# A new order of units in a block-sorted attention and gated MLP kernel

## The chip, the cores and the metric

The kernel runs on one core of a Trainium2 chip. The metric is device time in microseconds (us) of one execution. Before the change the median of three runs is 159.92 us (159.0 to 159.92). An engine here is one of TensorE (PE, with its weight loads as PEld), VectorE (DVE), ScalarE (ACT), GpSimd (POOL) and SyncE (SP, which in this kernel only starts DMAs). Each engine takes its instructions in the order in which the program wrote them, and waits on semaphores for what the others make.

## The reference

Two stages, four batches, eight heads, 768 tokens of 64 values, eight blocks of 96 tokens. The matrix P (8 x 8 for each batch and head) is normalised five times over rows and columns; K and V are mixed over blocks with P; each block of queries attends to its own mixed block. A gated MLP follows.

```python
for _ in range(5):                       # P: [B, H, 8, 8]
    P = np.exp(P - P.max(-1, keepdims=True))
    P = P / P.sum(-1, keepdims=True)
    P = P / P.sum(-2, keepdims=True)
k_sorted = einsum('bhij,bhjcd->bhicd', P, k_blocks)
v_sorted = einsum('bhij,bhjcd->bhicd', P, v_blocks)
attn = softmax(q_blocks @ k_sorted.T / 8)      # inside each block
x = (attn @ v_sorted) as [B, 768, 512]
h = relu(x @ w_in);  u, v = h[..., :512], h[..., 512:]
v_n = (v - mean(v)) / sqrt(var(v) + 1e-6)
gated = u * (w_spatial @ v_n + b_spatial)
out = gated @ w_out
```

## The kernel before

The whole program is one list of short units, the string `ORDER`. The program walks through the list and each word calls one function `u_<name>` with the arguments behind the colons. The place of a word in the list sets the place of its instructions in the queue of every engine that it uses; nothing reorders them later. The first number of most words is the PSUM bank that the unit writes (eight banks; a unit takes the bank and the one behind it), and the letter is the engine that empties it: A for ScalarE, D for VectorE, P for GpSimd.

The words, with the line of the work in the profile:

- `L:x:b`, `LH`: loads of q, k, v of batch b, and of the weights (`wv`, `wu`: the two halves of w_in; `ws`: w_spatial; `wo`: w_out). GpSimd writes them and casts float32 to bfloat16 on the way (lines 156, 165, 204 to 212).
- `SK`, `PR`, `P0`, `PC`, `PD`: P is normalised on a 32 x 64 tile, spread over 128 partitions on TensorE, and multiplied by a 0/1 mask into the mixing weights `pd` of a batch: for batch 0 by VectorE (`P0`, line 269), for the others by GpSimd (`PD`, line 281) from a copy (`PC`).
- `QT`, `KT`: q is transposed, k mixed and transposed, one pair of heads at a time (lines 324 and 339; a copy out of PSUM at line 108 or 110).
- `VT`, `VX`: batch 0 only. V is mixed like K (line 339), copied out, and turned back (line 378) into `vb`. The last argument of `VT` is 0 or 1 for one half of the blocks (64 columns) and 2 for all blocks at once (128 columns).
- `VM`, `VC`: the other batches. V is mixed with tokens on partitions into `vm` (line 390), and SyncE moves it into `vb` with one DMA for each block, four DMAs for each half of the blocks (line 405).
- `SC`, `AT`: scores and exp (lines 423 and 436), then attention times V (line 448) and the division (lines 459 and 460), for a batch, a pair of heads and a half `ih` of the blocks. `AT:...:P` sends the product through a ScalarE copy (line 456) to GpSimd.
- `XT`, `XX`: x is transposed, for batch 0 on TensorE, later by a DMA transpose of SyncE. `QX` (batches 2 and 3) arranges q, on VectorE (line 181) or GpSimd (line 179), and transposes it by such a DMA (line 183).
- `VP`, `LN`, `LA`: the v half of w_in, relu, mean and variance (lines 491, 114 or 116, 505, 506), the reciprocal root, and the normalisation on VectorE (line 525) or GpSimd (lines 521, 522).
- `UP`: the u half (line 536). `WS`: w_spatial transposed (line 297). `SP`, `SH`: the product with w_spatial (line 548; line 568 in halves), the bias (lines 554, 573) and the gate (lines 560, 577). `OP`, `OH`: w_out and the store (lines 597, 583).
- `DM`: products of a tile of zeros that nobody reads, early in the program (line 290).

`WT:q:2` is a copy of one element of the turned q of batch 2 on GpSimd (line 305). The loads of batch 3 stand behind it in GpSimd's queue, so they cannot start before that DMA transpose has landed. Buffers rotate: two each for q, k, v and `vb`, four for exp results, two for `z` (which `AT:...:P` shares), two and three for outputs.

Of the kernel before, what the change touches and what calls it, by code (L numbers as in the profile page):

```python
# [13 lines left out]


ORDER = """
IN SK:0 LH:q:0:0:4 L:k:0:0:128 ID MK SK:0 L:v:0:0:128 SK:0 QT:0:A:0:1:2 SK:0 QT:2:A:0:0:2 DM:0:12:64
LH:q:0:4:8 DM:1:12:64 SX L:wv DM:0:12:64 DM:1:12:64 SK:1 DM:0:12:64 DM:1:12:64 PR:0 P0:1:4:8 IV:1
P0:0:4:8 P0:1:0:4 P0:0:0:4 DM:7:5:384 KT:1:A:0:2:2 PC:A KT:3:A:0:3:2 VT:7:D:1:0 IV:0 VT:5:A:2:0
KT:1:D:0:1:2 VT:0:A:3:1 KT:6:A:0:0:2 VX:3:D:1:0 SC:1:0:1:0 VX:0:D:3:1 VX:3:D:2:0 QT:4:D:0:2:2  # L20
VT:7:A:0:1 VT:0:D:1:1 VT:1:A:0:0 SC:2:0:1:1 L:wu AT:6:D:0:1:0 L:ws SC:4:0:2:0 L:v:1:0:128 VX:0:D:0:1
VX:1:D:1:1 L:k:1:0:128 PD:2:4:8 PD:2:0:4 QT:2:A:0:3:2 VT:7:D:2:1 AT:4:D:0:2:0 VX:0:A:0:0 SC:2:0:0:0
AT:6:D:0:1:1 VT:0:A:3:0 SC:4:0:0:1 PD:1:0:4 AT:2:D:0:0:0 VX:0:D:3:0 SC:6:0:3:0 AT:4:D:0:0:1
SC:2:0:3:1 PD:1:4:8 SC:0:0:2:1 L:q:1:0:128 L:wo AT:6:D:0:3:0 VX:4:D:2:1 XT:2:A:0:1:0 XT:3:D:0:0:0
XT:7:D:0:0:1 AT:0:P:0:3:1 L:v:2:0:128 AT:4:D:0:2:1 WS:2:A:1 WS:3:A:3 VP:6:D:0:0:1 XT:0:A:0:1:1
VP:3:D:0:2 VM:4:A:1:1 L:k:2:0:128 VM:6:A:1:0 VP:0:D:0:5 PD:3:0:4 VM:4:A:1:2 VM:1:A:1:3 LN:0:0:3
VP:6:A:0:3:4 UP:1:A:0:0:0 L:q:2:0:128 KT:6:A:1:2:2 VC:1:0 VC:1:1 KT:4:D:1:3:2 WS:0:D:4 WS:1:A:2
LN:0:3:6 LA:P:0:2 LA:P:0:1 UP:2:A:0:0:1 WS:7:D:5 QT:4:A:1:1:2 KT:0:D:1:1:2 KT:2:A:1:0:2 LA:D:0:3
QT:6:D:1:0:2 QT:4:D:1:3:2 SC:0:1:1:0 UP:2:D:0:1:1 SC:0:1:0:0 LA:P:0:0 QT:6:A:1:2:2 AT:4:D:1:1:0
SC:0:1:0:1 AT:2:D:1:0:0 SC:6:1:1:1 WS:4:D:0 SC:0:1:3:0 PD:3:4:8 AT:2:D:1:0:1 SC:6:1:2:1 LA:D:0:5  # L30
SC:4:1:3:1 LA:P:0:4 BB AT:0:D:1:1:1 UP:2:A:0:1:0 AT:6:D:1:2:1 AT:4:P:1:3:1 SP:0:D:0:1 SC:4:1:2:0
AT:6:P:1:3:0 SP:2:P:0:0 XX:1:1 AT:6:D:1:2:0 XX:1:0 QX:D:2 VM:4:A:2:0 SP:0:D:0:3 KT:6:A:2:1:2
VM:4:A:2:3 SP:2:D:0:2 VM:4:A:2:1 VM:0:A:2:2 VP:6:A:1:4:5 UP:0:A:1:1:1 UP:4:A:1:0:0 KT:0:A:2:2:2
LN:1:4:6 VC:2:0 KT:6:D:2:3:2 KT:2:D:2:0:2 VP:4:D:1:2:3 SC:2:2:2:0 SC:6:2:0:0 VC:2:1 VP:0:D:1:0:1
WT:q:2:0 L:v:3:0:128 SC:6:2:3:1 SC:2:2:1:0 L:k:3:0:128 OP:4:A:0:2 AT:2:D:2:2:0 L:q:3:0:128 LN:1:0:4
LA:P:1:1 AT:0:D:2:0:0 LA:P:1:0 LA:D:1:5 OP:6:A:0:1 LA:P:1:4 AT:4:P:2:3:1 UP:2:D:1:0:1 SC:6:2:3:0
SC:0:2:0:1 LA:D:1:2 UP:4:A:1:1:0 AT:2:D:2:3:0 LA:P:1:3 AT:6:D:2:1:0 OP:0:D:0:0 SC:2:2:1:1 SC:6:2:2:1
SP:4:D:1:2 AT:6:P:2:1:1 SP:0:D:1:3 XX:2:0 AT:4:P:2:2:1 AT:6:D:2:0:1 SP:2:D:1:1 VM:4:A:3:3 XX:2:1
QX:P:3 SP:0:D:1:0 VM:4:A:3:2 VM:2:D:3:1 UP:6:A:2:1:0 VP:0:D:2:0:1 VM:6:A:3:0 KT:2:A:3:1:2
VP:4:A:2:2:3 UP:2:A:2:0:0 KT:4:D:3:0:2 KT:6:A:3:3:2 VC:3:1 LN:2:0:4 KT:0:A:3:2:2 VP:2:D:2:4:5  # L40
SC:4:3:0:1 LA:P:2:1 SC:0:3:2:0 VC:3:0 LA:P:2:2 UP:6:A:2:0:1 SC:2:3:3:1 SC:4:3:0:0 OP:0:A:1:0 LN:2:4:6
AT:2:D:3:2:0 LA:P:2:3 AT:6:D:3:3:1 LA:D:2:4 OP:4:A:1:2 AT:2:D:3:0:1 LA:P:2:5 AT:0:P:3:0:0
UP:6:D:2:1:1 LA:D:2:0 SC:2:3:2:1 SC:0:3:1:1 OP:4:A:1:1 AT:0:D:3:2:1 AT:2:D:3:1:1 SP:6:D:2:2
SC:2:3:3:0 XX:3:1 SC:0:3:1:0 SP:4:D:2:3 AT:0:P:3:3:0 AT:2:D:3:1:0 SP:6:P:2:1 XX:3:0 SP:4:D:2:0
UP:2:A:3:1:1 VP:4:D:3:4:5 OP:2:A:2:1 VP:4:D:3:2:3 LN:3:4:6 VP:2:A:3:0:1 UP:4:A:3:0:0 LA:P:3:5
LA:D:3:4 UP:6:A:3:1:0 LN:3:0:4 LA:D:3:3 LA:P:3:1 LA:P:3:0 UP:4:D:3:0:1 LA:D:3:2 OP:6:A:2:2 OP:4:D:2:0
SP:6:D:3:2 SP:4:D:3:0 SP:6:P:3:1 SH:4:D:3:3:1 SH:5:D:3:3:0 OH:7:A:3:3 OH:5:D:3:4 OH:4:A:3:0
OH:7:D:3:5 OH:5:A:3:1 OH:4:A:3:2
"""


# [593 lines left out]
```

## Time and profile before

| what | value |
|---|---|
| median of three runs | 159.92 us |
| the profiled execution | 159.92 us |
| its span, first to last instruction | 157.9 us |
| TensorE busy, granted clock | 141.8 us, 0.994 |
| VectorE, ScalarE, GpSimd busy | 117.4, 83.5, 53.8 us |
| loads by GpSimd: bytes written | 12.19 MB |
| DMAs by SyncE: bytes written | 13.06 MB |

The profiled execution took as long as the median of the runs, and 2.0 us of it lie outside the span. The loads of the first 57 us follow one another with little between them; these are the times at which they landed, from the time of issue and the time to landing in the DMA view: q of batch 0 (first half) 6.3 us, k 10.2, v 14.0, q (second half) 16.9, `wv` 19.4, `wu` 22.6, `ws` 27.6, then v, k, q of batch 1 at 31.5, 35.3 and 39.3, `wo` 43.4, and v, k, q of batch 2 at 49.4, 53.3 and 57.3.

### The profile page before, as it was taken

The numbers are of one execution on the slowest core, as the hardware profiler recorded it, in microseconds if no ns is written. First come the engines' busy times: TensorE is split into PE (matmuls) and PEld (weight loads), VectorE is DVE, ScalarE is ACT, GpSimd is POOL, SyncE is SP. The second block draws the span as 40 slices with busy tenths as digits, with TensorE's granted clock in tenths as the row PEclk, the third lists the DMA queues.
The fourth block names the chain that finished last, engine by engine and source line by source line (L and its number), as shares of the span: only waits on it lengthen the run. The fifth ranks groups of instructions, "written<-read, shape, count | busy, mean of one in ns | idle before, by whom it ended". The sixth has DMA issues, their size and how long they took to land.

```text
span 157.9 us, 3919 instructions
## 1 busy us (share of the span) xinstructions
PE 141.8 (90%) x1617; PEld 88.4 (56%) x1617; DVE 117.4 (74%) x231; ACT 83.5 (53%) x127; POOL 53.8 (34%) x78
## 2 busy tenths in 40 slices
PE   0399989999999999999799979999999999999880
PEld 0397878656766665645456644655566545555330
DVE  3775888699896698589566999775688679659830
ACT  3234989788887345757455343787751234410140
POOL 7961930758200350420830660062202401500400
PEclk9999999999999999999999999999999999999997
DMA  2999999999999999899999969741554503051073
GB/s 13 198 204 204 207 212 207 204 205 206 247 273 209 201 171 186 162 113 210 234 295 248 130 116 189 120 90 52 217 157 76 100 4 133 0 199 66 0 266 135
DMA packets 36689, 25.49 MB, mean 161 GB/s; under 512 B 16576, under 2 KB 33472, under 8 KB 36672
## 3 DMA queue, kind: packets, MB, share of 16 engines
q0 software_dynamic: 14864, 12.19, 50.0%
q1 hardware_dynamic: 21808, 13.06, 35.3%
q8 instruction: 12, 0.20, 0.4%
q14 instruction: 5, 0.04, 0.1%
HBM read 24.78 MB, written 6.29 MB: 197 GB/s over the span
## 4 chain that ended last, share of the span: by engine, by line
PE 61%; DMA 14%; DVE 12%; issue 4%; SPq 3%; ACT 2%; POOL 0%; DVEq 0%; ACTq 0%; POOLq 0%
PE ps L548 14%; PE ps L536 10%; PE ps L491 10%; DMA vb<-vm 10%; PE ps L597 8%; PE ps L448 4%; DVE z L554 4%; PE ps L339 3%; PE ps L290 3%; DMA q_in<-in_q_dram 3%; PE ps L423 3%; SPq L405 3%; DVE gt L560 2%; DVE x_sb L460 1%; DMA out_dram<-oh_sb 1%
## 5 line engine op out<-in xcount | busy, mean ns | idle before, releaser
L548 PE MATMUL ps<-wspT,v_sb 128*128 128x384 bf16 x180 | 31.2, 326 | 0.0
L436 ACT ACTIVATE ex<-ps 96x768 bf16<-96x768 f32 x32 | 24.5, 807 | 11.1 <-PE ps L423 11.1
L491 PE MATMUL ps<-w_in_sb,xT 128*128 128x512 bf16 x96 | 22.7, 379 | 1.2 <-DVE z L554 1.2
L536 PE MATMUL ps<-xT,w_in_sb 128*128 128x384 bf16 x128 | 23.0, 326 | 0.3 <-DVE x_sb L460 0.3
L548 PEld LDWEIGHTS <-v_sb 128*128 128x128 bf16 x180 | 17.0, 98 | 10.9
L460 POOL TENSOR_TENSOR x_sb<-xr,rec 96x512 bf16<-96x512 f32 x8 | 8.3, 1039 | 38.9 <-DVE rec L459 38.9
L554 DVE TENSOR_TENSOR z<-ps,b_bc 128x768 f32<-128x768 f32 x15 | 14.3, 954 | 5.4 <-PE ps L548 5.3
L505 DVE BATCH_NORM_STATS2 stats<-v_sb 128x6 f32<-128x512 bf16 x24 | 16.3, 678 | 2.6 <-ACT v_sb L114 2.3
L460 DVE TENSOR_TENSOR x_sb<-ps,rec 96x512 bf16<-96x512 f32 x24 | 16.5, 687 | 0.8
L597 PE MATMUL ps<-w_out_sb,gt 128*128 128x512 bf16 x72 | 16.9, 379 | 0.0
L536 PEld LDWEIGHTS <-w_in_sb 128*128 128x128 bf16 x128 | 12.1, 98 | 8.3 <-issue 0.3
L491 PEld LDWEIGHTS <-xT 128*128 128x128 bf16 x96 | 9.0, 98 | 11.0 <-issue 1.4
L522 POOL TENSOR_SCALAR v_sb<-v_sb,nm,rstd 128x512 bf16<-128x512 bf16 x15 | 12.1, 808 | 8.5 <-issue 5.4
L114 ACT ACTIVATE u_sb<-ps 128x768 bf16<-128x768 f32 x12 | 9.7, 810 | 8.6 <-PE ps L536 8.4
L560 DVE TENSOR_TENSOR gt<-z,u_sb 128x768 bf16<-128x768 f32 x12 | 13.6, 1137 | 0.4
L448 PE MATMUL ps<-vb,ex 96*128 96x65 bf16 x256 | 12.2, 193 | 1.4 <-DMA vb<-vm 1.4
L108 ACT CAST vm<-ps 128x768 bf16<-128x768 f32 x11 | 8.5, 803 | 8.3 <-PE ps L390 8.3
L116 DVE TENSOR_SCALAR v_sb<-ps 128x1024 bf16<-128x1024 f32 (+1 forms) x9 | 9.9, 1101 | 3.8 <-PE ps L491 3.7
L448 PEld LDWEIGHTS <-ex 96*128 96x128 bf16 x256 | 10.1, 97 | 4.3 <-issue 1.6
L521 POOL TENSOR_SCALAR nm<-mv 128x1 f32<-128x1 f32 x15 | 2.9, 194 | 24.3 <-DVE mv L506 17.8
L108 ACT CAST kT<-ps 128x768 bf16<-128x768 f32 x10 | 8.0, 804 | 5.7 <-PE ps L339 5.7
L108 ACT COPY o_sb<-ps 128x1024 f32<-128x1024 f32 x7 | 7.1, 1012 | 6.8 <-PE ps L597 6.6
(91 smaller groups left out, 205.2 us busy)
## 6 DMA issues: line engine op xcount, KB each, us to landing
out_dram<-o_sb SPq DMA_DIRECT2D x9, 512.0 KB, 3.0
k_in<-in_k_dram POOLq DMA_DIRECT2D x4, 768.0 KB, 19.9
v_in<-in_v_dram POOLq DMA_DIRECT2D x4, 768.0 KB, 15.6
vb<-vm SPq DMA_DIRECT2D x24, 99.0 KB, 4.8
q_in<-in_q_dram POOLq DMA_DIRECT2D x3, 768.0 KB, 20.1
out_dram<-oh_sb SPq DMA_DIRECT2D x6, 256.0 KB, 2.1
wsp_nat<-in_moe_w_spatial_dram POOLq DMA_DIRECT2D x1, 1152.0 KB, 19.8
w_in_sb<-in_moe_w_in_dram POOLq DMA_DIRECT2D x2, 512.0 KB, 14.5
```

Of the source, the lines that this page charges most:

```text
L108: nc.scalar.copy(out=out, in_=in_)
L436: nc.scalar.activation(out=dst, in_=src, func=AF.Exp, scale=scale)
L448: nc.tensor.matmul(t[:, hh, ii * VW:ii * VW + D + 1], lhsT=e[:, c:c + 128], rhs=vb[b % 2][:, ih * NI + ii, 2 * hp + hh, 0:D + 1], start=Tr ...
L460: (nc.gpsimd if eng == "P" else nc.vector).tensor_mul(out=x_sb[:, hp].rearrange("p i (h d) -> p h i d", h=2), in0=tv[:, :, :, 0:D], in1=_r ...
L491: nc.tensor.matmul(t[:, x, :], lhsT=x_tile(b, n // 3)[:, kc, n % 3 * 128:(n % 3 + 1) * 128], rhs=w_in_sb[:, kc, DH:DFF], start=(kc == 0), ...
L505: nc.vector.bn_stats(out=stats, in_=v_sb[:, x, :])
L522: nc.gpsimd.tensor_scalar(out=v_sb, in0=v_sb, scalar1=nm[:, 0:1], scalar2=rs[:, n:n + 1], op0=ALU.add, op1=ALU.mult)
L536: nc.tensor.matmul(t[:, x, 0:HW], lhsT=w_in_sb[:, kc, mc * 128:(mc + 1) * 128], rhs=x_tile(b, ih)[:, kc], start=(kc == 0), stop=(kc == KC ...
L548: nc.tensor.matmul(t[:, x, 0:HW], lhsT=st["v_sb", b, n][:, mc * 128:(mc + 1) * 128], rhs=wspT[:, n, x * HW:(x + 1) * HW], start=(n == 0), ...
L554: nc.vector.tensor_add(out=z.rearrange("p (x c) -> p x c", x=2), in0=t[:, :, 0:HW], in1=b_bc.rearrange("p (x c) -> p x c", x=2),)
L560: eng.tensor_mul(out=gt, in0=z, in1=st["u", b, mc // 2][:, mc % 2])
L597: nc.tensor.matmul(t[:, x, :], lhsT=st["gt", b, mc][:, c * 128:(c + 1) * 128], rhs=w_out_sb[:, mc, :], start=(mc == 0), stop=(mc == FC - 1),)
```

## The change

Only the list changes; every unit's function stays as it is. The number of words goes from 282 to 278, because batch 0's V is mixed in four units of 128 columns (`VT:...:2`) in place of eight of 64. The dummy products are as many and as wide as before (72 of 64 columns and 5 of 384). In the first part GpSimd's queue has the weights `wv`, `wu`, `ws` first, then two mask products, then v and k of batch 1; before, v and k of batch 1 were ahead of all mask products. GpSimd loads v of batch 2 before its first `AT`, and k and q of batch 2 between normalisations of batch 0. From batch 1 on nearly every unit has another place. Twelve `AT` units go to GpSimd (before, eight) and twelve `LA` units (before, fifteen).

The stretches that the prediction speaks of (the diff takes out the whole old list and puts in the whole new one):

```diff
-IN SK:0 LH:q:0:0:4 L:k:0:0:128 ID MK SK:0 L:v:0:0:128 SK:0 QT:0:A:0:1:2 SK:0 QT:2:A:0:0:2 DM:0:12:64
-LH:q:0:4:8 DM:1:12:64 SX L:wv DM:0:12:64 DM:1:12:64 SK:1 DM:0:12:64 DM:1:12:64 PR:0 P0:1:4:8 IV:1
-P0:0:4:8 P0:1:0:4 P0:0:0:4 DM:7:5:384 KT:1:A:0:2:2 PC:A KT:3:A:0:3:2 VT:7:D:1:0 IV:0 VT:5:A:2:0
...
-LN:1:4:6 VC:2:0 KT:6:D:2:3:2 KT:2:D:2:0:2 VP:4:D:1:2:3 SC:2:2:2:0 SC:6:2:0:0 VC:2:1 VP:0:D:1:0:1
-WT:q:2:0 L:v:3:0:128 SC:6:2:3:1 SC:2:2:1:0 L:k:3:0:128 OP:4:A:0:2 AT:2:D:2:2:0 L:q:3:0:128 LN:1:0:4
-LA:P:1:1 AT:0:D:2:0:0 LA:P:1:0 LA:D:1:5 OP:6:A:0:1 LA:P:1:4 AT:4:P:2:3:1 UP:2:D:1:0:1 SC:6:2:3:0
...
-SP:4:D:1:2 AT:6:P:2:1:1 SP:0:D:1:3 XX:2:0 AT:4:P:2:2:1 AT:6:D:2:0:1 SP:2:D:1:1 VM:4:A:3:3 XX:2:1
-QX:P:3 SP:0:D:1:0 VM:4:A:3:2 VM:2:D:3:1 UP:6:A:2:1:0 VP:0:D:2:0:1 VM:6:A:3:0 KT:2:A:3:1:2
...
+IN LH:q:0:0:4 L:k:0:0:128 SK:0 ID MK L:v:0:0:128 SK:0 SK:0 SX QT:0:A:0:1:2 SK:0 LH:q:0:4:8 SK:1
+QT:2:D:0:0:2 DM:0:12:64 DM:1:12:64 DM:0:12:64 DM:1:12:64 DM:0:12:64 DM:1:12:64 IV:0 PR:0 L:wv
+P0:1:0:4 P0:0:0:4 DM:7:5:384 KT:2:A:0:0:2 P0:1:4:8 P0:0:4:8 PC:D KT:4:A:0:1:2 KT:6:D:0:3:2 VT:0:A:0:2
...
+KT:6:A:2:1:2 KT:2:A:2:0:2 KT:4:A:2:3:2 VP:0:D:1:4:5 VP:2:A:1:2:3 VP:0:A:1:0:1 VC:2:0 VC:2:1
+SC:2:2:3:1 SC:4:2:3:0 UP:6:A:1:1:0 LN:1:0:4 UP:0:D:1:1:1 SC:4:2:0:1 LA:D:1:3 SC:2:2:2:1 WT:q:2:0
+L:v:3:0:128 OP:6:A:0:2 LA:P:1:0 AT:4:D:2:3:0 L:k:3:0:128 L:q:3:0:128 AT:0:P:2:3:1 LA:D:1:2 LN:1:4:6
+LA:P:1:5 OP:2:D:0:0 LA:D:1:1 AT:0:P:2:0:1 LA:D:1:4 AT:4:P:2:2:1 OP:6:D:0:1 SC:4:2:0:0 SC:2:2:1:0
+SP:0:D:1:3 SC:2:2:1:1 SC:6:2:2:0 UP:4:D:1:0:0 AT:2:D:2:1:1 AT:0:P:2:0:0 UP:6:A:1:0:1 AT:0:D:2:2:0
+AT:4:P:2:1:0 SP:2:D:1:1 VM:0:A:3:0 SP:4:D:1:0 VM:0:A:3:1 XX:2:1 KT:2:D:3:3:2 SP:6:D:1:2 VM:0:A:3:2
+VP:2:A:2:4:5 UP:0:A:2:1:1 XX:2:0 LN:2:4:6 VP:6:D:2:0:1 QX:P:3 VM:0:A:3:3 UP:2:A:2:0:0 LA:D:2:4
...
```

More of the change, by code (lines that the diff above doesn't have):

```diff
@@ L16 @@
 ORDER = """
-IN SK:0 LH:q:0:0:4 L:k:0:0:128 ID MK SK:0 L:v:0:0:128 SK:0 QT:0:A:0:1:2 SK:0 QT:2:A:0:0:2 DM:0:12:64
-LH:q:0:4:8 DM:1:12:64 SX L:wv DM:0:12:64 DM:1:12:64 SK:1 DM:0:12:64 DM:1:12:64 PR:0 P0:1:4:8 IV:1
-P0:0:4:8 P0:1:0:4 P0:0:0:4 DM:7:5:384 KT:1:A:0:2:2 PC:A KT:3:A:0:3:2 VT:7:D:1:0 IV:0 VT:5:A:2:0
-KT:1:D:0:1:2 VT:0:A:3:1 KT:6:A:0:0:2 VX:3:D:1:0 SC:1:0:1:0 VX:0:D:3:1 VX:3:D:2:0 QT:4:D:0:2:2
-VT:7:A:0:1 VT:0:D:1:1 VT:1:A:0:0 SC:2:0:1:1 L:wu AT:6:D:0:1:0 L:ws SC:4:0:2:0 L:v:1:0:128 VX:0:D:0:1
@@ L22 @@
[L22 to L33, printed above, removed]
@@ L34 @@
-LN:1:4:6 VC:2:0 KT:6:D:2:3:2 KT:2:D:2:0:2 VP:4:D:1:2:3 SC:2:2:2:0 SC:6:2:0:0 VC:2:1 VP:0:D:1:0:1
-WT:q:2:0 L:v:3:0:128 SC:6:2:3:1 SC:2:2:1:0 L:k:3:0:128 OP:4:A:0:2 AT:2:D:2:2:0 L:q:3:0:128 LN:1:0:4
-LA:P:1:1 AT:0:D:2:0:0 LA:P:1:0 LA:D:1:5 OP:6:A:0:1 LA:P:1:4 AT:4:P:2:3:1 UP:2:D:1:0:1 SC:6:2:3:0
-SC:0:2:0:1 LA:D:1:2 UP:4:A:1:1:0 AT:2:D:2:3:0 LA:P:1:3 AT:6:D:2:1:0 OP:0:D:0:0 SC:2:2:1:1 SC:6:2:2:1
-SP:4:D:1:2 AT:6:P:2:1:1 SP:0:D:1:3 XX:2:0 AT:4:P:2:2:1 AT:6:D:2:0:1 SP:2:D:1:1 VM:4:A:3:3 XX:2:1
-QX:P:3 SP:0:D:1:0 VM:4:A:3:2 VM:2:D:3:1 UP:6:A:2:1:0 VP:0:D:2:0:1 VM:6:A:3:0 KT:2:A:3:1:2
@@ L40 @@
[L40 to L45, printed above, removed]
@@ L46 @@
-LA:D:3:4 UP:6:A:3:1:0 LN:3:0:4 LA:D:3:3 LA:P:3:1 LA:P:3:0 UP:4:D:3:0:1 LA:D:3:2 OP:6:A:2:2 OP:4:D:2:0
-SP:6:D:3:2 SP:4:D:3:0 SP:6:P:3:1 SH:4:D:3:3:1 SH:5:D:3:3:0 OH:7:A:3:3 OH:5:D:3:4 OH:4:A:3:0
-OH:7:D:3:5 OH:5:A:3:1 OH:4:A:3:2
+IN LH:q:0:0:4 L:k:0:0:128 SK:0 ID MK L:v:0:0:128 SK:0 SK:0 SX QT:0:A:0:1:2 SK:0 LH:q:0:4:8 SK:1
+QT:2:D:0:0:2 DM:0:12:64 DM:1:12:64 DM:0:12:64 DM:1:12:64 DM:0:12:64 DM:1:12:64 IV:0 PR:0 L:wv
+P0:1:0:4 P0:0:0:4 DM:7:5:384 KT:2:A:0:0:2 P0:1:4:8 P0:0:4:8 PC:D KT:4:A:0:1:2 KT:6:D:0:3:2 VT:0:A:0:2
@@ new lines @@
+KT:2:D:0:2:2 SC:4:0:0:1 VT:6:D:1:2 L:wu VT:0:A:2:2 QT:2:A:0:3:2 VX:4:D:0:1 L:ws QT:6:D:0:2:2
+SC:0:0:1:1 PD:1:0:4 VX:4:D:0:0 VX:5:A:1:1 VX:2:D:2:1 VX:3:D:2:0 VT:6:A:3:2 AT:0:D:0:0:1 PD:2:0:4
+L:v:1:0:128 L:k:1:0:128 SC:4:0:2:1 AT:2:D:0:1:1 SC:6:0:3:1 VX:0:D:3:0 SC:4:0:2:0 IV:1 PD:3:4:8
+L:q:1:0:128 PD:3:0:4 VX:1:D:3:1 L:wo AT:2:D:0:2:1 SC:6:0:3:0 AT:0:D:0:3:1 SC:4:0:0:0 PD:1:4:8
+AT:6:D:0:2:0 SC:2:0:1:0 VX:4:D:1:0 XT:0:A:0:1:0 XT:1:D:0:1:1 AT:2:D:0:0:0 L:v:2:0:128 AT:6:P:0:3:0
+PD:2:4:8 AT:4:D:0:1:0 VP:0:A:0:5 VP:6:D:0:3:4 XT:0:A:0:0:0 XT:4:A:0:0:1 UP:2:A:0:1:1 WS:0:D:0
@@ new lines @@
+VM:6:A:1:0 VP:4:A:0:2 VM:2:D:1:1 VM:0:A:1:3 VM:6:A:1:2 LN:0:3:6 VP:4:D:0:0:1 KT:2:D:1:2:2 LA:P:0:3
+KT:6:A:1:3:2 UP:0:A:0:0:1 LN:0:0:3 UP:6:A:0:0:0 LA:P:0:4 KT:0:D:1:0:2 QT:4:A:1:3:2 QT:2:D:1:2:2
+L:k:2:0:128 LA:P:0:1 KT:6:A:1:1:2 QT:0:D:1:1:2 QT:4:A:1:0:2 L:q:2:0:128 SC:2:1:3:1 WS:7:D:4 WS:6:D:1
+VC:1:1 SC:4:1:1:1 SC:0:1:0:1 LA:P:0:5 WS:7:D:3 UP:2:A:0:1:0 AT:4:D:1:3:1 AT:0:D:1:1:1 SC:6:1:3:0
+WS:2:A:5 WS:3:D:2 AT:4:D:1:0:1 LA:P:0:0 BB SC:6:1:2:1 LA:P:0:2 SC:0:1:0:0 VC:1:0 AT:2:D:1:3:0
+SC:6:1:2:0 AT:4:D:1:2:1 SC:0:1:1:0 AT:2:P:1:0:0 SP:6:D:0:3 XX:1:1 AT:2:P:1:2:0 VM:0:A:2:2 SP:4:P:0:2
@@ new lines @@
+VM:0:A:2:3 AT:2:D:1:1:0 XX:1:0 QX:D:2 SP:6:P:0:0 VM:2:A:2:1 VM:0:A:2:0 SP:4:D:0:1 KT:0:A:2:2:2
+KT:6:A:2:1:2 KT:2:A:2:0:2 KT:4:A:2:3:2 VP:0:D:1:4:5 VP:2:A:1:2:3 VP:0:A:1:0:1 VC:2:0 VC:2:1
[3 more added lines that the diff above has]
+SP:0:D:1:3 SC:2:2:1:1 SC:6:2:2:0 UP:4:D:1:0:0 AT:2:D:2:1:1 AT:0:P:2:0:0 UP:6:A:1:0:1 AT:0:D:2:2:0
@@ new lines @@
+AT:4:P:2:1:0 SP:2:D:1:1 VM:0:A:3:0 SP:4:D:1:0 VM:0:A:3:1 XX:2:1 KT:2:D:3:3:2 SP:6:D:1:2 VM:0:A:3:2
+VP:2:A:2:4:5 UP:0:A:2:1:1 XX:2:0 LN:2:4:6 VP:6:D:2:0:1 QX:P:3 VM:0:A:3:3 UP:2:A:2:0:0 LA:D:2:4
+KT:0:A:3:0:2 VC:3:0 KT:6:A:3:2:2 KT:4:D:3:1:2 VP:2:D:2:2:3 SC:4:3:1:0 VC:3:1 SC:6:3:0:0 UP:0:A:2:0:1
+SC:2:3:3:0 SC:4:3:2:0 OP:6:A:1:0 AT:2:D:3:0:0 LA:P:2:5 AT:0:P:3:1:0 UP:4:A:2:1:0 AT:2:D:3:3:0
+LN:2:0:4 LA:D:2:0 LA:D:2:2 LA:P:2:1 AT:6:P:3:2:0 OP:0:D:1:2 SC:2:3:2:1 LA:D:2:3 SC:4:3:1:1 OP:6:A:1:1
+XX:3:0 AT:4:D:3:1:1 AT:0:P:3:2:1 SP:2:D:2:2 SC:0:3:0:1 SC:4:3:3:1 SP:6:D:2:0 AT:4:P:3:3:1 SP:0:P:2:1
@@ L49 @@
+AT:6:D:3:0:1 XX:3:1 UP:4:A:3:0:0 SP:0:D:2:3 VP:4:D:3:0:1 UP:0:A:3:1:0 OP:6:D:2:0 VP:0:D:3:4:5
+VP:6:A:3:2:3 OP:0:A:2:1 LN:3:4:6 LN:3:0:4 LA:D:3:3 LA:P:3:5 LA:P:3:4 LA:D:3:2 UP:6:A:3:0:1
+UP:4:A:3:1:1 LA:D:3:1 LA:D:3:0 OP:0:D:2:2 SP:4:D:3:2 SP:0:D:3:0 SP:4:P:3:1 SH:0:D:3:3:1 SH:1:D:3:3:0
+OH:0:D:3:4 OH:1:D:3:5 OH:4:A:3:3 OH:0:A:3:0 OH:1:A:3:1 OH:4:A:3:2
 """
```

## The prediction

> **What bounds the kernel now.** I read the page's totals and slices first, then TensorE's waits.
>
> ```profile
> span 157.9 us, 3919 instructions
> ...
> PE 141.8 (90%) x1617; PEld 88.4 (56%) x1617; DVE 117.4 (74%) x231; ACT 83.5 (53%) x127; POOL 53.8 (34%) x78
> ...
> PE   0399989999999999999799979999999999999880
> ```
>
> ```profile
> PE ps L324 <- DMA q_in<-in_q_dram: 6.3, 1, 6.3
> PE ps L448 <- DMA vb<-vm: 1.4, 3, 0.6
> PE ps L491 <- DVE z L554: 1.2, 1, 1.2
> PE ps L583 <- POOL gt L560: 0.6, 1, 0.6
> ```
>
> TensorE starts when q lands (6.3 us) and then hardly stops until 153.2 us. The changed list holds the same products, so its time is the same work plus the waits that the new places make. An order can gain only from the waits and lose without limit.
>
> **The work.** I price each unit's TensorE share by the chain of waits: 0.24 us for an AT (8 products in 0.48 us for two units), 0.25 for an SC, 0.43 for a KT or QT, 0.33 for a VM, 0.86 for one tile of VP, 1.30 for a UP, 1.95 for an SP, 1.73 for an OP. Four VT of 128 columns (0.43) replace eight of 64 (0.22): 1.72 against 1.76, nothing. From the first K product (13.43 us) to the end the list holds 129.7 us before and after. Where a stretch took longer than its sum I say it "lost" time.
>
> **Stage one, 13.4 to 51 us.** Up to the first SP the old list has 32.0 us of TensorE work and reached it at 50.76: 5.3 us lost, mostly at PSUM banks that wait for ScalarE and VectorE. I laid the new units on the queues with the rows of before (ScalarE copy 0.80, exp 0.81, VectorE copy 0.95, VX 0.41, AT 0.89) and followed each bank. VT in one go saves copying: 3 x 0.80 + 0.95 = 3.35 us against 5 x 0.49 + 3 x 0.55 = 4.10. QT:2 moves from ScalarE to VectorE between the end of the normalisation (11.69) and the first P0 (12.45): 0.95 us, so P0 starts at 12.64, 0.2 late, hidden by the five dummies of 384 columns that run to 13.50; without them 0.2 us. The first VM comes at about 32.3 with 15.9 us of work behind it (before: 31.55 with 14.9), which is 0.2 us better. It can't come before v lands (31.5), k and q hold the next steps at 35.3 and 39.3, and none of these loads comes earlier: GpSimd now issues v and k at about 16.7 and 17.6 instead of 8.66 and 9.53, but the loads queued ahead of them end at 27.65, so nothing runs dry. The same holds for the moved v, k and q of batch 2 (issued about 24, 39 and 41, the queue ahead of them full until 43, 49 and 53). SX ahead of q's second half delays its issue by 0.63 us and its landing not at all.
>
> For batch 1 `b_bc` (384 KB, 8.0 us to land) now stands between the two halves of VC, and VC starts 1.0 us later, since VM:2:D waits in VectorE's queue behind the statistics of VP:4:A:0:2. The second half lands about 49.3 to 50 (before 47.4), and TensorE wants it at 48.5. Behind it stand SC, AT and SP, but ScalarE is busy without a break from 42.6 to 52, and its exp frees SP's bank only at 51.0 anyway. So SP starts at 51.0 with 32.2 us done, level with before. Cost zero; between -0.5 and +1.0.
>
> **The second wait for `vb`, 51 to 77 us,** decides. These rows of the timeline are of before: SyncE, then GpSimd, then TensorE (start, duration, instruction).
>
> ```profile
> 58.98 4.53 SPq L183 DMA_TRANSPOSE qX<-qx  x1
> 63.61 7.22 SPq L405 DMA_DIRECT2D vb<-vm  x8
> ```
>
> ```profile
> 64.91 0.18 POOL L305 COPY gate<-qX 1x1 bf16<-1x1 bf16 x1 [6.87 <-DMA qX<-qx]
> 65.43 0.95 POOL L156 DMA_DIRECT2D v_in<-in_v_dram  x1 [0.35 <-issue]
> 66.40 0.88 POOL L156 DMA_DIRECT2D k_in<-in_k_dram  x1
> 67.26 0.88 POOL L156 DMA_DIRECT2D q_in<-in_q_dram  x1
> ```
>
> ```profile
> 73.09 0.65 PE L448 MATMUL ps<-vb,ex 96*128 96x65 bf16 x16
> 73.57 1.89 PE L597 MATMUL ps<-w_out_sb,gt 128*128 128x512 bf16 x8
> 75.30 0.23 PE L448 MATMUL ps<-vb,ex 96*128 96x65 bf16 x2
> 75.96 0.19 PE L448 MATMUL ps<-vb,ex 96*128 96x65 bf16 x1 [0.43 <-DMA vb<-vm]
> 76.75 0.31 PE L448 MATMUL ps<-vb,ex 96*128 96x65 bf16 x5 [0.60 <-DMA vb<-vm]
> ```
>
> q of batch 2 lands at 57.3, is arranged and turned, and only then SyncE reaches the eight `vb` transfers. The first four landed 2.7 to 3.1 us after issue; the next four, beside the load of v, 7.0 to 8.3, the last at 76.71. TensorE came to the first AT of the second half at 75.3 and lost 1.03 us.
>
> After, this chain begins with the same load. QX ends 0.4 us later (its first copy stood 1.13 us beside GpSimd's gate product, and that one ends 0.2 later; AT:2:D:1:1:0 stands ahead of it), so the transfers start about 64.0. But TensorE comes earlier: from SP at 51.0 to AT:0:P:2:3:1 the new list has 4 SP, 3 AT, 4 VM, 4 KT, 3 pairs of VP, 4 SC, 2 UP and one OP = 22.05 us (before 24.3, with two OP and three UP) plus 0.3 lost as before = 73.4. Behind the waiting AT stands the whole of TensorE's queue. Bounds: if the last transfer lands as late as before plus 0.4 (77.1), the wait is 3.7 us; if all eight land 3.1 us after issue, 72, there is none. Something speaks for a landing earlier than 77.1: k and q of batch 3 now stand behind LA:P:1:0 on GpSimd, which waits for LN:1:0:4 (about 71.7), so only v loads beside `vb`; in the stretch before, 1.9 MB moved from 65 to 76.7, of which 0.79 (vb) and 0.77 (v) account for 1.56, and the rest at some 220 GB/s is 1.5 us. I take 76.2, nearer to the row: wait 2.8, **1.8 us more than before**.
>
> Here a rule can be set against the rows. The Trainium skill, "DMA: Bandwidth & Descriptors", section "Queues, rings and completion order", has each DMA engine take turns between queues packet by packet. By it the last four transfers (0.40 MB) would be done when as much of v has moved: 0.79 MB at the 127 GB/s of that stretch, an estimate of 6.2 us from 66.5, landing 72.7, no wait, and a total 2.8 us lower than mine. The rows show 7.0 to 8.3 us, so I go by them.
>
> **VectorE behind GpSimd, 82 to 97 us.** DVE and POOL in the timeline of before:
>
> ```profile
> 90.02 0.94 DVE L554 TENSOR_TENSOR z<-ps,b_bc 128x768 f32<-128x768 f32 x1
> 91.00 3.10 DVE L560 TENSOR_TENSOR gt<-z,u_sb 128x768 bf16<-128x768 f32 x1
> 94.02 0.94 DVE L554 TENSOR_TENSOR z<-ps,b_bc 128x768 f32<-128x768 f32 x1
> ```
>
> ```profile
> 90.39 2.90 POOL L179 TENSOR_SCALAR qx<-q_in 128x1536 bf16<-128x1536 bf16 x2
> ```
>
> A gate product of 0.96 us took 3.10 beside QX:P:3, the next z freed the bank late, and VP lost 1.16 us. After, GpSimd reaches QX right after the x of AT:4:P:2:1:0, just when VectorE has the gate of SP:2:D:1:1. That gate, z and gate of SP:4 and the copy of KT:2:D:3:3 come 1.9 us late, and VP:2:A:2:4:5 waits for that copy's bank about 1.5 us: **+0.3**. Bounds: 0 to 1.9 us of wait, -1.2 to +0.7.
>
> **The rest.** From there both lists lost about half a us in 43 us. The four additional AT on GpSimd (0.59 ScalarE, 0.20 VectorE, 1.04 GpSimd each) and OP copies on VectorE (three more, 1.22) lie beside TensorE work; the last transposes of x are ready about 127, VP:0:D:3:4:5 comes at 129; if they slip over 2 us TensorE waits. The last LA on GpSimd ends 1 us ahead of its product. The tail (SP D, D, P, SH, SH, six OH) has the same engines up to the copies of OH, whose last waits for an output buffer either way: 0, between -0.5 and +0.3.
>
> **Sum.** -0.2 + 0 + 1.8 + 0.3 + 0 = +1.9 us, on a span of 157.9: 159.8, and with the 2.0 us outside it **161.8 us**; the profiled execution equals the median, so that is the median's forecast too.
>
> **Rivals.** (1) The transfers are there when TensorE comes, because k and q of batch 3 no longer load beside them: it decides if the last lands before 73.4. Then -1.03 replaces +1.8: 159.0, and with the low ends of stage one (-0.5) and of QX (-1.2 in place of +0.3) 157.0, faster than before. For it: first-half transfers took 3 us; against: v still loads beside the second half. (2) The late k and q cost something themselves. If q needs 20.1 us again from an issue at 74, it lands at 94 instead of 85.5 (3.1 MB left to move at 250 GB/s), is turned by 102.5, and SC wants it at 105 to 107; 2 us later than that and it adds 2: 163.8. (3) The change gains nothing by its V in one go, since the loads set stage one: that is in the forecast; if instead banks set it, 0.75 us of copies go: 161.0.
>
> **Chances.** Forecast with its wait of 2 to 3.7 us, 161.0 to 162.7: 0.5. Rival 1 0.25, of which 0.1 falls under 158.3. Rival 2, or further waits of that kind, 0.17; the rest 0.08. This measurement can tell about 1% (1.6 us) from no change. Faster by over 1%: 0.10; within 1%: 0.39; slower by over 1%: 0.51. The range reaches from rival 1's upper part to rival 2: 158.6 to 164.0.
>
> **What would show it.** Right: the waits list has `vb` for L448 at 2 to 3.7 us in one place near 73 to 77, a gate product of about 3 us on VectorE beside `qx`, the first SP at 51 +- 0.5 and the tail from SP to the end 18.7 us long. Wrong: no `vb` wait there, or TensorE at the first SP off by over 1 us, or a wait for `qX` near 105.
>
> One rule may worsen a long wait: "TensorE: Matmul & The Clock Gate", Part 1, has the clock halved after an idle window of about 3.4 us. No wait here after the start is longer than 1.2 us and the granted clock is 0.994, so nothing shows it; at my upper bound of 3.7 it could add what a stretch at half clock costs.

## The result, and the profile after

The changed kernel takes 167.46 us (median of four runs, 166.15 to 168.34), the kernel before 159.68 (four runs, 159.0 to 159.92): a ratio of 1.049, 95% interval 1.040 to 1.057. The forecast was 161.8 with a range of 158.6 to 164.0. It had the sign and missed the size by 5.7 us. All ratios here leave out disturbed runs, so a median over all runs of a kernel can stand above what its ratio says.

The profiled execution of the changed kernel took 168.34 us with a span of 166.4, 8.5 us more than before. Line numbers are one lower than in the kernel before. First the page's totals and slices of the changed kernel (a slice is 4.2 us):

```profile
span 166.4 us, 3820 instructions
...
PE 143.8 (86%) x1569; PEld 89.2 (54%) x1569; DVE 116.5 (70%) x229; ACT 83.4 (50%) x127; POOL 56.8 (34%) x77
...
PE   0389899999979999998808996999999999999880
...
PEclk9999999999996999999975999999999999999999
```

TensorE stands still for a whole slice (the second 0 of its row, 83.2 to 87.4 us), and its granted clock falls twice: to 6 tenths at 49.9 to 54.1 us, and to 7 and 5 tenths at 83.2 to 91.5. The waits list of the changed kernel (engine, tile and line of the waiting instruction, releaser; then us in total, times, the longest) names the first:

```profile
PE ps L422 <- DVE o_sb L109: 5.5, 1, 5.5
PE ps L447 <- DMA vb<-vm: 1.6, 3, 0.8
PE ps L490 <- DVE kT L109: 1.3, 1, 1.3
```

The first line is new and the prediction has no word of it. A product of `SC` waited for VectorE to copy an output block out of its bank, and that copy, in VectorE's timeline of the changed kernel (start, duration, instruction, idle time before it and its releaser), had waited itself:

```profile
86.66 1.23 DVE L109 COPY o_sb<-ps 128x1024 f32<-128x1024 f32 x1 [7.22 <-DMA out_dram<-o_sb]
```

There are two output buffers. `OP:6:D:0:1` is the third `OP` of batch 0 and needs the buffer of the first, whose store SyncE issued at 75.58 us. VectorE came to that copy at 79.4, as TensorE was ending the third block; the store landed at 86.6, 11.0 us after its issue. VectorE stood for 7.22 us, and TensorE behind it for 5.5. In TensorE's timeline of the changed kernel the stall has a tail:

```profile
82.04 0.38 PE L422 MATMUL ps<-qX,kT 64*96 64x96 bf16 x8
87.94 0.56 PE L422 MATMUL ps<-qX,kT 64*96 64x96 bf16 x8 [5.52 <-DVE o_sb L109]
88.43 2.74 PE L535 MATMUL ps<-xT,w_in_sb 128*128 128x384 bf16 x8
90.97 1.09 PE L447 MATMUL ps<-vb,ex 96*128 96x65 bf16 x16
```

The `UP` took 2.74 us where others take 1.47, the pair of `AT` 1.09 where others take 0.65: 1.7 us lost. The table by stretches of the changed kernel (stretch, length, busy time of PE, PEld, DVE, ACT, POOL, then granted clock, DMA share and GB/s) has the clock beside it, 0.50 just there:

```profile
84.00:86.00 2.00, 0.00 (x0) 0.00 (x0) 0.00 (x0) 0.00 (x0) 0.00 (x0) 0.78 1.18 268
86.00:92.00 6.00, 4.06 (x33) 2.62 (x33) 3.76 (x4) 0.81 (x1) 0.00 (x0) 0.50 0.74 169
92.00:98.00 6.00, 6.00 (x53) 3.80 (x50) 4.30 (x9) 2.68 (x4) 3.97 (x4) 1.00 0.49 87
```

The other low clock is at the first `SP`, again in TensorE's timeline of the changed kernel:

```profile
48.59 0.19 PE L447 MATMUL ps<-vb,ex 96*128 96x65 bf16 x1 [0.85 <-DMA vb<-vm]
49.01 0.31 PE L447 MATMUL ps<-vb,ex 96*128 96x65 bf16 x5 [0.23 <-DMA vb<-vm]
...
50.64 3.70 PE L547 MATMUL ps<-wspT,v_sb 128*128 128x384 bf16 x12
```

The `SP` started where the prediction put it (51.0), but took 3.70 us for 2.12, and the `AT` behind it 0.54 for 0.41: another 1.7 us.

The sum: the stall 5.5, the low clock after it 1.7, the low clock at 50 us 1.7, the second `vb` wait 0.6 less than before (0.47 for 1.03): 8.3 of the 8.5 us.

### The profile page after: what moved, and what is told of

Its sections match the earlier page's. It is cut to its first block, busy times and chain, and to the rows that moved or that the text cites. A ratio compares the mean times of both kernels' runs of the same rounds, so it can differ in the third digit from the quotient of the medians.

```text
span 166.4 us, 3820 instructions
## 1 busy us (share of the span) xinstructions
PE 143.8 (86%) x1569; PEld 89.2 (54%) x1569; DVE 116.5 (70%) x229; ACT 83.4 (50%) x127; POOL 56.8 (34%) x77
## 4 chain that ended last, share of the span: by engine, by line
PE 56%; DMA 23%; DVE 10%; issue 3%; ACT 3%; POOL 2%; DVEq 0%; ACTq 0%; SPq 0%; POOLq 0%
PE ps L547 13%; PE ps L490 12%; PE ps L535 11%; DMA vb<-vm 8%; PE ps L596 7%; DMA q_in<-in_q_dram 7%; DMA out_dram<-o_sb 7%; PE ps L447 4%; PE ps L422 3%; DVE z L553 3%; DVE gt L559 2%; PE ps L338 2%; PE ps L377 1%; PE ps L389 1%; DMA out_dram<-oh_sb 1%
## 5 line engine op out<-in xcount | busy, mean ns | idle before, releaser
L547 PE MATMUL ps<-wspT,v_sb 128*128 128x384 bf16 x180 | 33.0, 337 | 0.0
L459 POOL TENSOR_TENSOR x_sb<-xr,rec 96x512 bf16<-96x512 f32 x12 | 12.5, 1048 | 45.6 <-DVE rec L458 36.2
L535 PE MATMUL ps<-xT,w_in_sb 128*128 128x384 bf16 x128 | 24.3, 339 | 0.0
L113 ACT ACTIVATE u_sb<-ps 128x768 bf16<-128x768 f32 x14 | 11.3, 809 | 10.3 <-PE ps L535 10.0
L459 DVE TENSOR_TENSOR x_sb<-ps,rec 96x512 bf16<-96x512 f32 x20 | 13.7, 687 | 0.7
L422 PEld LDWEIGHTS <-kT 64*96 64x96 bf16 x256 | 7.9, 122 | 9.6 <-issue 8.1
L521 POOL TENSOR_SCALAR v_sb<-v_sb,nm,rstd 128x512 bf16<-128x512 bf16 x12 | 9.7, 810 | 8.9 <-ACT rstd L512 4.4
L109 DVE COPY o_sb<-ps 128x1024 f32<-128x1024 f32 x5 | 6.1, 1220 | 8.4 <-DMA out_dram<-o_sb 7.2
L455 ACT COPY xr<-ps 96x520 f32<-96x520 f32 x12 | 6.9, 586 | 8.0 <-PE ps L447 7.8
L115 DVE TENSOR_SCALAR v_sb<-ps 128x1024 bf16<-128x1024 f32 x7 | 8.6, 1224 | 3.4 <-PE ps L490 3.4
```

The source lines that it names most:

```text
L113: nc.scalar.activation(out=out, in_=in_, func=AF.Relu)
L422: nc.tensor.matmul(t[0:BLK, hh, ii * 128:ii * 128 + BLK], lhsT=kT[rows, i * BLK:(i + 1) * BLK], rhs=rhs, start=True, stop=True,)
L459: (nc.gpsimd if eng == "P" else nc.vector).tensor_mul(out=x_sb[:, hp].rearrange("p i (h d) -> p h i d", h=2), in0=tv[:, :, :, 0:D], in1=_r ...
L535: nc.tensor.matmul(t[:, x, 0:HW], lhsT=w_in_sb[:, kc, mc * 128:(mc + 1) * 128], rhs=x_tile(b, ih)[:, kc], start=(kc == 0), stop=(kc == KC ...
L547: nc.tensor.matmul(t[:, x, 0:HW], lhsT=st["v_sb", b, n][:, mc * 128:(mc + 1) * 128], rhs=wspT[:, n, x * HW:(x + 1) * HW], start=(n == 0), ...
```

## The experiments

The theory from this trace: **A**, the store wait with the low clock after it is the loss. Its rivals: **B**, the `vb` wait of batch 1 with the low clock at 50 us matters as much or more; **C**, the time belongs to the new order of stage one (V in one go, loads behind mask products). The runs were on different chips, where the kernel before had medians from 159.3 to 160.7, so times are compared by their ratio to it.

### A third output buffer

```diff
-        o_sb = moe.tile([128, DM], FP32, name="oh_sb", tag="oh", bufs=3)
+        o_sb = moe.tile([128, 2, DM], FP32, name="oh_sb", tag="o", bufs=3)[:, 0]
...
-        o_sb = moe.tile([128, 2, DM], FP32, name="o_sb", tag="o", bufs=2)
+        o_sb = moe.tile([128, 2, DM], FP32, name="o_sb", tag="o", bufs=3)
```

> The changed kernel with a third output buffer (the OH units take theirs from the same three, so nothing else grows); every engine's order stays as it is. Theory A, the store: the third OP copy waited 7.2 us on VectorE for the store of the first, TensorE lost 5.5 us behind it and 1.7 us more at half clock (UP 2.74 instead of 1.50, sixteen AT products 1.09 instead of 0.65). All of it goes: about 160.3 us. Rival B, the wait only moves: TensorE then comes to the late q and k of batch 3 and waits there: 164 or more. Rival C, the granted clock halves there anyway: 162.

Measured: 160.36 us, ratio to before 0.999 (0.991 to 1.007), span 158.8. The wait for the store is gone from VectorE and TensorE, though the store itself took as long (10.8 us). VectorE, then TensorE, in this version:

```profile
78.07 1.23 DVE L109 COPY o_sb<-ps 128x1024 f32<-128x1024 f32 x1 [0.16 <-PE ps L596]
```

```profile
50.52 2.12 PE L547 MATMUL ps<-wspT,v_sb 128*128 128x384 bf16 x12
...
94.69 1.90 PE L490 MATMUL ps<-w_in_sb,xT 128*128 128x512 bf16 x8 [2.56 <-DMA xT<-x_sb]
```

By the ratios this one edit takes back the whole loss of 5%: theory A holds. But the sum has other terms. In this execution the first `SP` took 2.12 us too, though its `vb` waits before it were nearly the same (0.77 and 0.26), so 1.7 us of the gain is the low clock at 50 us, which this edit does not touch. On the other side a new wait of 2.6 us came (`VP` for `xT`, at 94.7). The store wait with its low clock, 7.2 us, is the part that the edit is shown to take away.

The same edit in the kernel before:

> Control: the kernel before with the same third output buffer. Its third OP copy came 8 us after the second and waited for no store, so 159.7 us, no change. A gain here would mean that the buffer helps by itself and not by undoing the change.

Measured: 160.50 us, ratio 1.0005 (0.992 to 1.009). SyncE and VectorE in the kernel before, and its DMA view from 73 to 76 us:

```profile
74.32 0.42 SPq L605 DMA_DIRECT2D out_dram<-o_sb  x1
82.56 1.22 DVE L110 COPY o_sb<-ps 128x1024 f32<-128x1024 f32 x1 [0.26 <-PE ps L597]
```

```profile
out_dram<-o_sb SPq DMA_DIRECT2D x1, 512.0 KB, 7.0
```

The third copy came at 82.6 us and the store had landed at 81.3, so the buffer was free with 1.3 us to spare.

### The bias load behind the second half of V

```diff
-WS:2:A:5 WS:3:D:2 AT:4:D:1:0:1 LA:P:0:0 BB SC:6:1:2:1 LA:P:0:2 SC:0:1:0:0 VC:1:0 AT:2:D:1:3:0
+WS:2:A:5 WS:3:D:2 AT:4:D:1:0:1 LA:P:0:0 VC:1:0 BB SC:6:1:2:1 LA:P:0:2 SC:0:1:0:0 AT:2:D:1:3:0
```

> The changed kernel with the load of b_bc behind the second half of batch 1's vb transfers, as before, instead of ahead of them. Theory A: the wait for vb at 47.7 to 49.0 (1.08 us) shrinks to about 0.5 and the halved clock at 50.6 to 54.1, which cost about 1.8 us (first SP 3.70 instead of 2.12, first AT 0.54 instead of 0.41), does not come: 165 us. Rival: the clock halves for another reason (the many short products from 40 to 50, bound by ScalarE): 167 us and a slow first SP as in the changed kernel.

Measured: 162.07 us, ratio 1.009 (1.001 to 1.017): 5.4 us better, far more than expected. TensorE's timeline of this version:

```profile
49.54 2.11 PE L547 MATMUL ps<-wspT,v_sb 128*128 128x384 bf16 x12
...
74.75 0.19 PE L447 MATMUL ps<-vb,ex 96*128 96x65 bf16 x1 [1.79 <-DMA vb<-vm]
```

The `vb` wait of batch 1 and the low clock at 50 us are gone, as theory B says of its share. But TensorE, earlier by that, now meets the second `vb` wait in the size that the prediction gave it (1.79 and 0.52 us), a low clock after it (two `OP` 2.5 us each for 1.9, the `AT` between them 1.09 for 0.65: 1.7 us lost), and comes to the third output block only at 81.3. The store, issued 1.9 us earlier and landed within 8.0, is just done then (copy at 81.87, no wait for it). So what this edit gains is the same store wait with its low clock, missed by a hair; its gain at 50 us and its loss at the second `vb` wait nearly cancel. The losses are not a sum of independent parts: what delays TensorE ahead of a fixed transfer is given back at the wait.

Both edits together:

> Both edits of the two runs ahead of this one. If the two losses are all that the new order adds: 158 us, level with or under the kernel before. If the order loses elsewhere too: 160 or more.

Measured: 159.64 us, ratio 0.993 (0.983 to 1.004): level with the kernel before, as the first expectation says, though 1.6 us above its 158 us. The `vb` wait at 74 to 75 us stays (1.9 us in two).

### Why the store took 11 us

```diff
-L:v:3:0:128 OP:6:A:0:2 LA:P:1:0 AT:4:D:2:3:0 L:k:3:0:128 L:q:3:0:128 AT:0:P:2:3:1 LA:D:1:2 LN:1:4:6
+L:v:3:0:128 OP:6:A:0:2 L:k:3:0:128 L:q:3:0:128 LA:P:1:0 AT:4:D:2:3:0 AT:0:P:2:3:1 LA:D:1:2 LN:1:4:6
```

In the changed kernel the loads of k and q of batch 3 are issued at 73.44 and 74.38 us, just ahead of the store. The DMA view of the changed kernel, 74.2 to 76.5 us (the last column is the time to landing):

```profile
k_in<-in_k_dram POOLq DMA_DIRECT2D x1, 768.0 KB, 13.3
...
out_dram<-o_sb SPq DMA_DIRECT2D x1, 512.0 KB, 11.0
```

> The changed kernel with the loads of k and q of batch 3 written ahead of LA:P:1:0 on GpSimd, nothing else. They should be issued near 70 us in place of 73.4 and 74.4. The question is why the store of OP:0:2 took 11.0 us to land. If it is because two fresh loads were issued just ahead of it, a part of them is done by 75.6 us, the store lands in 7 to 9 us as in the kernel before (7.0), VectorE waits 2 to 5 us in place of 7.2, and the time is 163 to 165. If the store takes 11 us whatever the loads do, it stays at 167 to 168. If the earlier loads slow the vb transfers, a vb wait near 75 grows over 0.5 us.

Measured: 163.40 us (four runs, 161.19 to 164.65), ratio 1.029 (1.021 to 1.036), within the first expectation. The ratio is less certain than its interval says: the two lowest runs, 161.19 and 162.52, would give 1.017 by themselves, and the profiled execution is the 161.19. The same view of this version, and its VectorE and TensorE:

```profile
out_dram<-o_sb SPq DMA_DIRECT2D x1, 512.0 KB, 7.1
```

```profile
81.01 1.23 DVE L109 COPY o_sb<-ps 128x1024 f32<-128x1024 f32 x1 [3.16 <-DMA out_dram<-o_sb]
82.29 0.38 PE L422 MATMUL ps<-qX,kT 64*96 64x96 bf16 x8 [1.45 <-DVE o_sb L109]
```

The loads are now issued at 68.0 and 68.8 us. The store takes 7.1 us, VectorE waits 3.2 and TensorE 1.5, and the clock stays at 1.0 behind so short a stall. The `OP` in its new place makes this rest of the wait. The other versions tell how much the loads add: the first store took 7.0, 7.0, 7.1, 7.1, 7.2 and 7.9 us where the loads were issued 4.4 us or more ahead of it (the kernel before with two and with three buffers, this one, and the three below that hold this edit beside others), and 8.0, 8.2, 9.2, 9.2, 9.4, 9.8, 10.8 and 11.0 in those with them issued 2.1 and 1.2 us ahead. So they go with 1 to 4 us more; why 4 in the changed kernel and 1 with the bias load moved stays open.

### The third OP later, with two buffers

```diff
-... AT:4:P:2:2:1 OP:6:D:0:1 SC:4:2:0:0 SC:2:2:1:0
+... AT:4:P:2:2:1 SC:4:2:0:0 SC:2:2:1:0
...
-AT:4:P:2:1:0 SP:2:D:1:1 VM:0:A:3:0 SP:4:D:1:0 VM:0:A:3:1 XX:2:1 ...
+AT:4:P:2:1:0 SP:2:D:1:1 VM:0:A:3:0 OP:6:D:0:1 SP:4:D:1:0 VM:0:A:3:1 XX:2:1 ...
```

> The changed kernel with the third OP, OP:6:D:0:1, moved about 9 us later in the list, ahead of SP:4:D:1:0; still two output buffers. If the store wait with what follows it is the loss, the copy now comes at about 87 us when the store has landed, no wait is left, and the time is that of the version with three buffers: 160.4, at most 161.5. If the place of that OP matters for something else (the gate and the v half behind it), it stays over 163.

Measured: 163.33 us, ratio 1.025 (1.022 to 1.027): the store wait is gone, but 3 of its 7 us are back. SyncE, then TensorE, in this version:

```profile
73.84 15.47 SPq L604 DMA_DIRECT2D out_dram<-o_sb  x3
89.42 5.52 SPq L189 DMA_TRANSPOSE xT<-x_sb  x2
```

```profile
95.64 1.46 PE L490 MATMUL ps<-w_in_sb,xT 128*128 128x512 bf16 x3 [2.87 <-DMA xT<-x_sb]
```

The moved copy's store is the third in SyncE's queue, and it waits there until the copy ends at 88.9. The transposes of x stand behind it and start at 89.42, where the version with three buffers starts them at 84.5; `VP` waits 2.87 us for them, and the clock is 0.60 from 95 to 98 us. With three buffers `VP` waited for `xT` too, 2.56 us, but it began at 94.69, 0.95 us earlier, and the clock stayed at 1.00. So of the 2.3 us between the two spans (161.1 and 158.8) about 1 is the later transposes, and the rest, behind the start of `VP`, goes with the low clock. An edit that cures one queue was paid for in another: the expectation had not followed SyncE.

### Keeping TensorE busy through the stall

```diff
-SP:0:D:1:3 SC:2:2:1:1 SC:6:2:2:0 UP:4:D:1:0:0 ...
+SP:0:D:1:3 SC:2:2:1:1 DM:4:28:384 SC:6:2:2:0 UP:4:D:1:0:0 ...
```

> The changed kernel with 28 products of zeros of 384 columns (about 4.6 us at 0.16 to 0.18 each, by the SP rows) put ahead of the product that stalls at 82.4 us; nobody reads them. They do no work but keep TensorE busy in the stall. If the clock at 86 to 92 us was halved because TensorE stood idle before, the granted clock stays at 1.0 there, UP takes 1.47 in place of 2.74 us and AT 0.65 in place of 1.09: 1.7 us less, 165.7. If the stall is worth only itself and the low clock had another cause, 167.5, and with a stall shorter than the products the time grows by the difference.

Measured: 164.71 us, ratio 1.033 (1.027 to 1.039): 2.7 us faster than the changed kernel by doing 4.7 us of useless work. TensorE's timeline of this version, and its table by stretches:

```profile
81.61 4.72 PE L289 MATMUL ps<-warm 128*128 128x384 bf16 x28
...
86.57 1.47 PE L535 MATMUL ps<-xT,w_in_sb 128*128 128x384 bf16 x8
```

```profile
86.00:92.00 6.00, 6.00 (x71) 3.93 (x69) 4.43 (x9) 2.68 (x4) 1.50 (x2) 1.00 0.72 166
```

The `UP` behind the stall runs at full clock. So the low clock there came from TensorE's idleness, and its price is 1.7 us; that the remaining 1 us comes from the store, which landed in 9.2 us here, is not shown.

This agrees with the Trainium skill, "TensorE: Matmul & The Clock Gate", Part 1, which has the clock halved after an idle window of about 3.4 us. Other low clocks here do not follow that rule as simply: 0.60 behind one wait of 2.87 us (the third `OP` later), 0.59 behind 1.79 and 0.52 (the bias load moved), and at 50 us in the changed kernel no wait ahead was longer than 0.85 us.

### Stage one undone, part by part

V of batch 0 in halves again (`VT:0:A:0:2` becomes `VT:0:A:0:0 VT:1:A:0:1`, and so for the other three), with a third output buffer:

> The changed kernel with a third output buffer (160.4 measured), and batch 0's V mixed in eight units of 64 columns as before the change, in place of four of 128. The prediction had VT in one go save 0.75 us of copies and 0.04 us of TensorE, hidden behind the loads but for 0.2 us. So 160.4 to 160.6. If copies set stage one, 161.1; the first VM, which starts at 31.6 us, would then start 0.5 to 0.7 later.

Measured: 162.83 us, ratio 1.016 (1.009 to 1.023), more than either expectation. In stage one the halves cost little: the first `AT` that waits for an exp starts at 24.55 us in place of 24.11, 0.4 later. The rest lies at 74.8 us, where TensorE waited 1.5 and 0.6 us for `vb` (0.7 with V in one go), and in a clock of 0.66 from 75 to 80.

Loads of v and k of batch 1 ahead of the mask products again, with a third output buffer:

```diff
-SC:0:0:1:1 PD:1:0:4 VX:4:D:0:0 ... AT:0:D:0:0:1 PD:2:0:4
-L:v:1:0:128 L:k:1:0:128 SC:4:0:2:1 ...
+SC:0:0:1:1 L:v:1:0:128 L:k:1:0:128 PD:1:0:4 VX:4:D:0:0 ... AT:0:D:0:0:1 PD:2:0:4
+SC:4:0:2:1 ...
```

> The changed kernel with a third output buffer (160.4 measured), and v and k of batch 1 loaded ahead of the first mask products on GpSimd, undoing that part of the change. The prediction had nothing from it: the loads queued ahead end at 27.65 us, so these land as before (31.5, 35.3). So 160.4 within the measurement, and first VM at 31.6 plus or minus 0.3. If the mask products become late by it, TensorE waits for them with some tenths of a us.

Measured: 159.34 us, ratio 0.993 (0.988 to 0.998). The first `VM` starts at 31.63 us, against 31.57 with the loads behind the mask products: that part of the change brought nothing and cost nothing in stage one. C falls as the cause of the 7.8 us.

### All edits together

> The changed kernel with three edits: a third output buffer, the second half of batch 1's VC ahead of BB, and k and q of batch 3 ahead of LA:P:1:0. The first two together measured 159.6. The third brings at most 1 us if k and q of batch 3 were late in any way, and costs up to 1 if they slow the vb transfers: 158.6 to 160.6, where the kernel before has 160.0.

Measured: 159.07 us, ratio 0.996 (0.993 to 1.000).

> The changed kernel with four edits: a third output buffer, the second half of batch 1's VC ahead of BB, k and q of batch 3 ahead of LA:P:1:0, v and k of batch 1 ahead of the first mask products. The first three measured 0.996 of the kernel before, the first and the fourth 0.993. If the gains are of different waits (vb at 48, loads beside the stores, the first VM), they add: 0.987 to 0.993, some 158 us. If they are one and the same slack, 0.993 to 0.998.

Measured: 162.38 us (six runs, 159.87 to 163.22), ratio 1.002 (0.996 to 1.008). The gains do not add: the trace has 1.2 and 0.6 us of `vb` wait at 73.7 and 74.5 again.

> The kernel with the four edits, and batch 0's V in eight units of 64 columns again. The prediction put V in one go at 0.2 us (0.7 if copies set stage one): then this is 0.1 to 0.7 us above the kernel with the four edits. With two of the edits missing, the halves had cost some 2.5 us, and the trace had there a vb wait of 1.5 us at 74.8 and a low clock after it. If these came from the V units themselves, it is 2 to 3 us above; if they came from the place where the vb transfers fell, under 1.

Measured: 162.86 us, ratio 1.008 (1.000 to 1.015): 0.5 us above the kernel with the four edits by the medians, 0.9 by the ratios, which rest on two runs each, and the intervals overlap. So V in one go is worth under 1 us, not clear of the noise. That the rest of what the halves had cost with three buffers alone came from where the `vb` transfers fell (from 64.05 us on, against 62.92 with V in one go) is argued from the traces. No version was faster than the kernel before by more than 1%.

## Why the prediction was wrong

**The step that failed** is in "The rest": "OP copies on VectorE (three more, 1.22) lie beside TensorE work". I priced these copies by their duration and never asked what each waits for. The rows of before were enough to see it. The store of the first output block took 7.0 us there; the new list has 3.8 us between that store's issue and the third block (75.58 to 79.4). That alone is a VectorE wait of 3.2 us and, as measured with the loads earlier, a TensorE stall of 1.5. The other 4 us of this store's landing go with k and q of batch 3 being loaded just ahead of it. I had seen that these loads come later, and asked only what that does to `vb` and to q itself (rival 2), not to a store beside them. With three buffers the time is 160.4. The two waits also hang together: had TensorE stood at `vb` for the 2.8 us of the forecast, the third block would have come some 2.3 us later and a store of 7.0 us would have held VectorE for only about 0.9, by my estimate; with the bias load moved, TensorE did stand 2.3 us there and lost 1.7 by its clock, and the store wait was none.

**The clock.** I named the rule on idle windows, tied it to a `vb` wait of 3.7 us that I held unlikely, and gave it no price. It cost 1.7 us behind the store wait; a low clock cost 1.7 more at 50 us, where the rule does not explain it.

**Stage one.** The loads behind the mask products were worth nothing, as forecast, and V in one go was small (0.2 forecast, 0.4 in the trace). The first `SP` came at 50.64 (51 forecast), but that was partly luck. The cost "zero" of `b_bc` between the halves of `VC` was wrong: `vb` came late by 0.85 and 0.23 us as the landing times foretold. I had that hidden behind ScalarE, whose exp would free the bank of `SP` only at 51.0 anyway. But ScalarE stood too, for the scores behind that wait (0.81 us ahead of its exp at 49.73); with the bias load moved its exps ran through and `SP` started at 49.54. So the place of `b_bc` cost 1.1 us there.

**The second `vb` wait.** This term was mis-sized. Forecast: last landing 76.2, TensorE there at 73.4, wait 2.8. Measured: TensorE there at 74.85, since it had lost 1.7 us at 50 us, last landing 75.3, wait 0.47. With a full clock at 50 us and the same order up to `SP` (three buffers, k and q earlier, or the third `OP` later) TensorE came at 73.0 to 73.1, near the forecast, and the wait was still only 0.3 to 0.7, for the last transfer landed at 73.4 to 73.7. What I had wrong is which transfers run beside the load of v. Before, that load was issued at 65.43, behind the third of the eight, and the last four took 7.0 to 8.3 us. In the changed kernel it comes here (GpSimd's timeline):

```profile
68.77 0.94 POOL L155 DMA_DIRECT2D v_in<-in_v_dram  x1 [0.34 <-issue]
```

By then six of the eight had been issued, from 64.64 on, and the seventh went out at 68.86; these seven landed in 2.8 to 3.7 us, and only the eighth, issued at 69.50, took 5.8. So rival 1 was nearer in size, though its reason (k and q no longer beside them) left out that v comes late too. Over all the versions above with a full clock at 50 us the waits at 73 to 76 lay between 0.3 and 2.7 us (2.3 with the bias load moved, where TensorE came earlier): the term was of the right kind and far less certain than 2 to 3.7.

The Trainium skill, "DMA: Bandwidth & Descriptors", "Queues, rings and completion order", by my estimate put the last landing at 72.7; the rows, 75.3 in the changed kernel and 73.7 with three buffers, lie between that and the 76.2 from the rows of before.

**VectorE behind GpSimd.** Right. The timeline of the changed kernel, VectorE and GpSimd:

```profile
96.90 2.89 DVE L559 TENSOR_TENSOR gt<-z,u_sb 128x768 bf16<-128x768 f32 x1
```

```profile
96.08 2.90 POOL L178 TENSOR_SCALAR qx<-q_in 128x1536 bf16<-128x1536 bf16 x2
```

The gate product took 2.89 us beside `qx`, and `VP` waited 1.3 (1.5 forecast, 1.2 before). There was no wait for q of batch 3 near 105 us, and from the first `SP` of the last batch to the end it took 18.8 us (18.7 forecast).

**The sum.** The forecast span was 159.8, the measured one 166.4: +5.5 (store wait) +1.7 and +1.7 (clock) -2.3 (`vb`) = 6.6, the whole difference. That these add up so well is partly luck, since 1.7 of it is the low clock at 50 us, which three of the four other versions with the same order up to there did not show. The range ended at 164.0 because the case "further waits of that kind" had no place and no price.

## What to carry to other kernels

When an order of work changes, follow every buffer that rotates: for each writer, set the time at which it comes against the landing of the transfer that frees its buffer, with the transfers that will then run beside it. Here two output buffers were enough with 1.3 us to spare, and cost 7 us when the third user came 3.8 us behind the first one's store in place of 8.3 and two loads moved in front of that store. A stall of TensorE of several us should be priced with what its clock costs afterwards (here 1.7 us behind 5.5, and some behind 2.87, none behind 1.45 or 2.56), and an instruction that is moved later must be followed through the queue of the DMAs that it feeds.
